# Start-up in half maxima with low parts last, rank products three units later, tokens picked inside the first expert's down stage

## The chip, the cores and the metric

One core of a Trainium2 chip runs the kernel in one launch. The metric is the device time of one execution in microseconds (us).

## The reference

Only the lines that set the work are kept. Q, K and V are 4 batches x 8 heads x 768 x 64. A row of Q sees only the rows of K whose nearest of 16 centroids is the same one. The result, 3072 tokens of 512 features, goes through a mixture of 16 experts in 4 groups (F = 1024), one expert per token.

```
q_assign = np.argmax(np.einsum('bhsd,hcd->bhsc', q_n, c_n), axis=-1)
k_assign = np.argmax(np.einsum('bhsd,hcd->bhsc', k_n, c_n), axis=-1)
mask = q_assign[:, :, :, None] == k_assign[:, :, None, :]
scores = np.where(mask, scale * np.matmul(q, k.transpose(0, 1, 3, 2)), -1e9)
attn = softmax(scores); x = attn @ v            # per head, then heads side by side
g_idx = np.argmax(x @ w_group, axis=1)          # group, then expert in the group
e_idx = np.argmax(xg @ w_expert[g], axis=1)
out[tok] = g_w * e_w * (np.maximum(x[tok] @ w1[g, e], 0.0) @ w2[g, e])
```

## The kernel before

Every number is split into a high and a low f16 part, so that a product is three matmuls (high by high, high by low, low by high). Four stages matter here.

**Start-up (lines 450 to 480).** Heads go in pairs; pair 0 is loaded first. `split` makes the high part of K and of Q on ACT (L178) and the low part on DVE (L187). The centroids are normalised, transposed on PE and split on DVE into CH and CL (L168, L169). `assign` multiplies the pair with CH and CL (L239, 72 matmuls) and finds the winning centroid of each row on DVE: L244 (maximum), L246, L247, L249, L251. `mask_now` transposes the resulting one-hot rows on PE (L276) and copies them into the operand tiles A, on ACT for Q (L278) and on DVE for K (L280). From then on the mask is part of the score product.

**Attention loop (lines 504 to 515).** 32 heads x 9 units. A **coarse** unit multiplies high parts only (L302, one bank of 512 columns) and DVE reduces it to row maxima (L305). When the 9 coarse units of a head are done, `rowmax` joins them (DVE L311, ACT L313), transposes the result on PE (L318 for heads 0 and 1) and writes it into A on ACT (L319). Only then can the head's **fine** units run: PE L342 and L343, exp on ACT (L347), low part of the exponentials on POOL (L349), products with V on PE (L368, L369) five units later. The coarse units run ahead of the fine ones by 13 units at first and by 18 later. A table of jobs keyed by unit number (`at`, `go`, `turn`) says when loads, splits, assignments, masks and routing of other heads are issued between units.

**Routing (lines 617 to 676).** At the end of each batch, `decide` chooses group and expert on DVE (L624 to L646), then counts ranks within the experts with 12 small matmuls on PE (L651 to L655), and turns them into positions on DVE (L658 to L663); POOL scatters token numbers and gates into `table` (L674). For batches 0 to 2 this runs as a job beside attention, and the value it yields (`yield PSM, 1, 1`) says how many units later it goes on. After batch 2 the first expert's known tokens are read from the table (tabA), cast to indices (DVE L838) and gathered (POOL L912). Batch 3 goes the way `early`, after attention.

**First expert (loop in the code below).** `part_a` runs the first expert on 288 tokens: eight up products (L950), then four down blocks d0 to d3 (L968, 24 matmuls each: 8 with hh and wh, 8 with hh and wl, 8 with hl and wh). Each up product yields once and each down block twice, after 12 and 24 matmuls; the loop counts those steps. At step `SLOTS` it issues `slots`: 6 f32 matmuls of `tb` (the table read back, SP L1084) by a permutation (L1114), which give the indices (DVE L1025) for the gathers of the next group of tokens (POOL L912). At step `SLT` it issues `tokens_b`: 48 matmuls that pick the expert's remaining tokens from batch 3 (L1096) and 6 f32 ones for their numbers (L1100); 128 tokens then follow as the second pass of this expert (L950).

Of the kernel before, what the change touches and what calls it, by code (L numbers as in the profile page):

```python
# [32 lines left out]
def attention(ctx, tc, qT, kT, vr, cen, R, DEN, cfg):  # L33
# [15 lines left out]
    AHEAD, AHEAD0 = 18, 13  # L49
# [116 lines left out]
    for j in range(2):  # L166
        r = slice(64 * j, 64 * j + 64)
        nc.vector.tensor_copy(out=CH[r, :, j], in_=cv[r, :, j])  # L168
        nc.vector.tensor_tensor(out=CL[r, :, j], in0=cv[r, :, j], in1=CH[r, :, j], op=ALU.subtract)  # L169


    def split(p, w, pool=False):
# [5 lines left out]
        nc.scalar.activation(out=hi, in_=x, func=AF.Copy, scale=SQ)  # L178
# [38 lines left out]
    def splitv(p, pool=False):  # L217
        x = st[p][2]
        vt = V[p % 4]
        nc.scalar.activation(out=vt[:, :, :, 64:128], in_=x, func=AF.Copy, scale=SQ)  # L220
        lo_part(vt[:, :, :, 0:64], x, vt[:, :, :, 64:128], pool)

    def assign(p, psum=None):
# [10 lines left out]
        for c in range(NCH):  # L234
            cs = slice(c * P, c * P + P)
            for t in range(2):
                hi, lo = st[p, t]
                for i, (a, m) in enumerate(((hi, CH), (hi, CL), (lo, CH))):
                    nc.tensor.matmul(out=sim[:, c, t], lhsT=a[:, cs], rhs=m[:, pr].rearrange("p h c -> p (h c)"), start=i == 0, stop=i == 2)  # L239
        sim = simt[:, 0:NCH * 4 * C].rearrange("p (g c) -> p g c", c=C)  # L240
        G = 4 * NCH
        yield
# [28 lines left out]
    def mask_now(h, pool):  # L271

        for t, dst in ((0, QA[h]), (1, KA[h])):
# [3 lines left out]
            if t == 0:  # L277
                nc.scalar.activation(out=dst[64:64 + C], in_=tp[64:64 + C, :S], func=AF.Copy, scale=-32768.0)  # L278
            else:
# [12 lines left out]
    def coarse(h, u, pool=(ps_c, "psc")):  # L292
# [6 lines left out]
        pc = pool[0].tile([P, 512], F32, name=pool[1])  # L299
        off = 0  # L300
# [6 lines left out]
    def rowmax(h):  # L307

        mp = cparts.pop(h)
        m7 = sm.tile([P, NCH], F32, name="m7")  # L310
        last["max"] = nc.vector.tensor_reduce(out=m7, in_=mp.rearrange("p j a x -> p (j a) x"), axis=AX.X, op=ALU.max)  # L311
        mh = ozs[0][:, 0, h, :, 64 + C] if h < 2 else sm.tile([P, NCH], F16, name="mh")
        nc.scalar.activation(out=mh, in_=m7, func=AF.Copy, scale=-1.0 / (SQ * SQ))  # L313
        if h < 2:

            tp = ps_f.tile([P, 512], F32, name="psf").bitcast(F16)
            for c in range(NCH):
                nc.tensor.transpose(out=tp[0:OZ, c * P:(c + 1) * P], in_=ozs[0][:, 0, h, c], identity=ident)  # L318
            nc.scalar.activation(out=QA[h][64:OZ], in_=tp[64:OZ, :S], func=AF.Identity, scale=oscale[64:OZ], bias=obias[64:OZ])  # L319
# [130 lines left out]
    split(0, 1)  # L450
    split(0, 0)
# [3 lines left out]
    run(assign(0, ps_f.tile([P, 512], F32, name="psf")))  # L455
    mask_now(0, (ps_o, "pso"))
    spread(0, (0,), part=(1,))
    banks = itertools.cycle(((ps_c, "psc"), (ps_f, "psf")))
    for u in range(9):
        coarse(0, u, next(banks))  # L460
    mask_now(1, (ps_o, "pso"))
    spread(0, (1,), part=(1,))
    run(rowmax(0))
# [5 lines left out]
    with tc.issue_after(last["mm"].ins), tc.issue_after(last["max"].ins):  # L469
        for u in range(AHEAD0 - 9):  # L470
            coarse(1, u, next(banks))
# [953 lines left out]
```

## Time and profile before

| | |
|---|---|
| median of 3 runs | 786.41 us (784.92 to 787.25) |
| profiled execution | 782.34 us, span of the core 780.6 us |
| PE busy | 733.3 us (94%) |
| PE weight loads | 626.5 us (80%, beside PE) |
| DVE busy | 612.0 us (78%) |
| POOL busy | 495.6 us (63%) |
| ACT busy | 466.8 us (60%) |
| DMA | 128.28 MB, mean 164 GB/s |

The span is the time on the core; the execution's own time is 1.74 us longer. A time of an instruction is its start from the span's beginning, and what stands in brackets behind it is the idle time of its engine just before it with what ended that. The clock column of the views by stretch is the clock granted to PE, where 1.00 is 2.4 GHz and 0.50 is 1.2 GHz.

### The profile page before, as it was taken

To read this page: it belongs to the slowest core of one execution; us is meant where nothing else is said; L and a number is where in the kernel's file an instruction comes from. 1 tells how busy PE (TensorE), PEld (TensorE's weight loads), DVE (VectorE), ACT (ScalarE), POOL (GpSimd) and SP (SyncE) were. 2 spreads that over 40 slices of the span, in tenths; PEclk is the share of its full clock that TensorE was granted. 3 is DMA by queue.
4 is the path that set the end of the run, shared out by engine and by line. 5 is a ranking of instruction groups with operands and counts; after the bars stand their busy time and mean duration, and the time that the engine had idled before them with its cause. 6 is when DMAs were issued, how large, how long until landed. Compare 5 with 4: busy or idle time off the path is not lost. (4 is left out here: it accounts for less than half of the span.)

```text
span 780.6 us, 26678 instructions
## 1 busy us (share of the span) xinstructions
PE 733.3 (94%) x11086; PEld 626.5 (80%) x11086; DVE 612.0 (78%) x1209; ACT 466.8 (60%) x910; POOL 495.6 (63%) x497
## 2 busy tenths in 40 slices
PE   5899999999999999998999799999999999999991
PEld 3677888878888788886878677887789999999991
DVE  5998879899798988988875465867789888888830
ACT  5567877768777687775895255444344444555530
POOL 9578787778977788776972445434564655565330
PEclk7899999999999999999999999999999999999996
DMA  8856534435344352223312397866688688889600
GB/s 244 204 144 168 148 102 119 137 94 148 104 119 134 94 149 68 55 94 127 92 30 84 85 313 239 272 224 217 209 265 257 218 259 277 285 255 300 194 32 17
DMA packets 80392, 128.28 MB, mean 164 GB/s; under 512 B 8851, under 2 KB 47251, under 8 KB 80264
## 3 DMA queue, kind: packets, MB, share of 16 engines
q1 hardware_dynamic: 74492, 113.12, 48.9%
q0 software_dynamic: 5616, 13.35, 4.9%
q8 instruction: 88, 1.44, 0.8%
q14 instruction: 40, 0.33, 0.1%
q10 hardware_dynamic: 156, 0.03, 0.0%
HBM read 93.20 MB, written 14.11 MB: 137 GB/s over the span
## 5 line engine op out<-in xcount | busy, mean ns | idle before, releaser
L349 POOL TENSOR_TENSOR pl<-p 128x512 f16<-128x512 f32 x278 | 287.3, 1052 | 84.9 <-ACT p L347 80.7
L305 DVE TENSOR_REDUCE mpart<-psc 128x1 f32<-128x512 f32 (+1 forms) x282 | 189.8, 682 | 35.0 <-PE psc L302 32.8
L347 ACT ACTIVATE p<-psf 128x512 f32<-128x512 f32 x288 | 168.7, 595 | 56.1 <-PE psf L343 49.1
L368 PE MATMUL pso<-V,p 128*128 128x65 f16 x1152 | 161.6, 193 | 0.0
L368 PE MATMUL pso<-V,pl 128*128 128x65 f16 x1152 | 161.2, 194 | 0.0
L369 PE MATMUL pso<-V,pl 128*128 128x64 f16 x1152 | 161.0, 191 | 0.0
L369 PE MATMUL pso<-V,p 128*128 128x64 f16 x1152 | 160.8, 191 | 0.0
L342 PE MATMUL psf<-A 82*128 82x384 f16 (+2 forms) x576 | 143.7, 275 | 4.2 <-ACT p L347 2.8
L343 PE MATMUL psf<-B 128*128 128x384 f16 (+2 forms) x576 | 143.7, 274 | 0.0
L369 PEld LDWEIGHTS <-p 128*128 128x128 bf16 x1152 | 112.6, 98 | 21.4 <-issue 0.2
L368 PEld LDWEIGHTS <-p 128*128 128x128 bf16 x1152 | 112.2, 97 | 9.3 <-issue 1.4
L369 PEld LDWEIGHTS <-pl 128*128 128x128 f16 x1152 | 112.8, 98 | 0.7 <-issue 0.4
L302 PE MATMUL psc<-A 80*128 80x512 f16 (+1 forms) x376 | 108.4, 330 | 5.1 <-DVE mpart L305 3.3
L368 PEld LDWEIGHTS <-pl 128*128 128x128 f16 x1152 | 111.2, 97 | 0.3
L953 DVE SCALAR_TENSOR_TENSOR hl<-psh,hh 128x160 f16<-128x160 f32 (+14 forms) x136 | 49.9, 370 | 58.6 <-ACT hh L952 50.4
L952 ACT ACTIVATE hh<-psh 128x160 f16<-128x160 f32 (+14 forms) x136 | 46.6, 347 | 65.7 <-PE psh L950 64.3
L950 PE MATMUL psh<-xT,wh0a 128*128 128x288 f16 (+7 forms) x512 | 74.7, 255 | 0.0
L1011 POOL DMA_INDIRECT out_dram<-y,ri x32 | 38.5, 1203 | 55.1 <-ACT y L1010 48.8
L912 POOL DMA_INDIRECT xg<-xbuf,ri x32 | 43.5, 1359 | 39.8 <-PE psm L922 25.7
L343 PEld LDWEIGHTS <-B 128*128 128x128 f16 x576 | 56.6, 98 | 13.7 <-issue 5.3
L950 PE MATMUL psh<-xT,wh0b 128*128 128x272 f16 (+6 forms) x448 | 65.2, 254 | 0.9 <-ACT xT L924 0.5
L342 PEld LDWEIGHTS <-A 82*128 82x128 f16 x576 | 55.5, 98 | 12.0 <-DMA A<-mr 0.7
(308 smaller groups left out, 1776.9 us busy)
## 6 DMA issues: line engine op xcount, KB each, us to landing
st<-w SPq DMA_DIRECT2D x128, 512.0 KB
B<-parts SPq DMA_DIRECT2D x64, 192.0 KB
kx<-kT SPq DMA_DIRECT2D x16, 384.0 KB
qx<-qT SPq DMA_DIRECT2D x16, 384.0 KB
vx<-vr SPq DMA_DIRECT2D x16, 384.0 KB
A<-parts SPq DMA_DIRECT2D x32, 192.0 KB
xbuf<-xs SPq DMA_DIRECT2D x4, 1536.0 KB
A<-mk SPq DMA_DIRECT2D x56, 24.0 KB
```

What stands on the lines that cost most here:

```text
L302: last["mm"] = nc.tensor.matmul(out=pc[:, off:off + k1 - k0], lhsT=QA[h % 8][0:80, c * P:(c + 1) * P], rhs=KA[h % 8][0:80, k0:k1], start=T ...
L305: nc.vector.tensor_reduce(out=(mp[:, 0, 0:1], mp[:, :, 1], mp[:, 1, 0:1])[i], in_=pc.rearrange("p (a x) -> p a x", a=n), axis=AX.X, op=ALU ...
L342: nc.tensor.matmul(out=o, lhsT=KA[h % 8][0:82, ks], rhs=QA[h % 8][0:82, q0:q1], start=True, stop=False)
L343: nc.tensor.matmul(out=o, lhsT=KBs[h][:, ks], rhs=QBs[h][:, q0:q1], start=False, stop=True)
L347: cfg["exp"] = nc.scalar.activation(out=p32, in_=pf, func=AF.Exp, scale=QK / (SQ * SQ))
L349: lo = (nc.vector if u in (EARLY if h < 2 else DVE_LO[h % 8] if h < NH - 2 else DVE_END) else nc.gpsimd).tensor_tensor(out=pl, in0=p32, in ...
L368: nc.tensor.matmul(out=O[:, col:col + 65], lhsT=p[:, bs], rhs=vh, start=c == 0 and q == 0 and i == 0, stop=False, skip_group_check=True)
L369: nc.tensor.matmul(out=O[:, col:col + 64], lhsT=p[:, bs], rhs=vl, start=False, stop=c == NCH - 1 and i == 1, skip_group_check=True)
L912: self.got = nc.gpsimd.indirect_dma_start(out=xg[0:n].rearrange("p a d -> p (a d)"), out_offset=None, in_offset=bass.IndirectOffsetOnAxis( ...
L950: self.mm = nc.tensor.matmul(out=ph[:, 0:M], lhsT=w[:, k, fs], rhs=xT[:, a, k], start=i == 0, stop=i == 3 * KD - 1)
L952: nc.scalar.activation(out=hh[:, f], in_=ph[:, 0:M], func=AF.Relu)
L953: self.ev = nc.vector.scalar_tensor_tensor(out=hl[:, f], in0=ph[:, 0:M], scalar=0.0, in1=hh[:, f], op0=ALU.max, op1=ALU.subtract)
```

## The change

The low parts of pair 0 go behind the four CH and CL instructions on DVE. `assign(0)` does its products in the order high by CH, high by CL, low by CH, K ahead of Q, and its chain of maxima once for each head of the pair, on half the columns each, with the mask transposes of head 0 between. Six matmuls on a zero tile (128x512) follow its products, and two more stand ahead of each of the first five coarse units: 16 matmuls and their weight loads are new on PE. Of head 0 only five coarse units come ahead of the loop; its row maximum is taken in two halves, and the first three fine units need the first half only. The other coarse units, `assign(1)`, and the masks of heads 2 and 3 become jobs of the first units; the number of coarse units ahead is 5 at first and grows by one with each unit up to 18. The mask of K for head 1 goes from DVE to ACT. The high parts made by `split` and `splitv` inside the loop are put behind the latest exp on ACT.

The rank products of batches 0 to 2 come three units after their inputs were issued instead of one. `SLOTS` goes from 11 to 13 and `SLT` from 13 to 8.

```diff
-    AHEAD, AHEAD0 = 18, 13
+    AHEAD = 18
...
-        nc.vector.tensor_tensor(out=CL[r, :, j], in0=cv[r, :, j], in1=CH[r, :, j], op=ALU.subtract)
+        last["cl"] = nc.vector.tensor_tensor(out=CL[r, :, j], in0=cv[r, :, j], in1=CH[r, :, j], op=ALU.subtract)
...
-        nc.scalar.activation(out=hi, in_=x, func=AF.Copy, scale=SQ)
+        with tc.issue_after(cfg["exp"].ins) if "exp" in cfg else ExitStack():
+            nc.scalar.activation(out=hi, in_=x, func=AF.Copy, scale=SQ)
...
+        if p == 0:
+
+            prods = [(c, t, i) for i in range(3) for t in (1, 0) for c in range(NCH)]
+        else:
+            prods = [(c, t, i) for c in range(NCH) for t in range(2) for i in range(3)]
+        for c, t, i in prods:
...
+        yield
+        if p == 0:
+
+            sim = simt[:, 0:NCH * 4 * C].rearrange("p (g h c) -> p g h c", h=2, c=C)
+            G = 2 * NCH
+            for h in range(2):
+                mx = sm.tile([P, 2 * G], F32, name="mx")[:, 0:G]
+                nc.vector.tensor_reduce(out=mx, in_=sim[:, :, h], axis=AX.X, op=ALU.max)
...
+                yield
+            return
...
             if t == 0:
                 nc.scalar.activation(out=dst[64:64 + C], in_=tp[64:64 + C, :S], func=AF.Copy, scale=-32768.0)
+            elif h == 1:
+                nc.scalar.activation(out=dst[64:64 + C], in_=tp[64:64 + C, :S], func=AF.Identity, scale=mscale[64:64 + C], bias=mbias[64:64 + C])
...
-    def coarse(h, u, pool=(ps_c, "psc")):
+    def coarse(h, u, pool=(ps_c, "psc"), idle=0):
...
+        for _ in range(idle):
+
+            nc.tensor.matmul(out=pc, lhsT=wz[:, 0:P], rhs=wz, start=True, stop=True)
...
-    def rowmax(h):
+    def rowmax(h, c0=0, c1=NCH):
...
-    split(0, 1)
-    split(0, 0)
+    with tc.issue_after(last["cl"].ins):
+        split(0, 1)
+        split(0, 0)
...
-    run(assign(0, ps_f.tile([P, 512], F32, name="psf")))
+    first = assign(0, ps_f.tile([P, 512], F32, name="psf"))
+    next(first)
+    with tc.issue_after(last["sim"].ins):
+        warm(6)
+    next(first)
     mask_now(0, (ps_o, "pso"))
+    run(first)
     spread(0, (0,), part=(1,))
     banks = itertools.cycle(((ps_c, "psc"), (ps_f, "psf")))
-    for u in range(9):
-        coarse(0, u, next(banks))
+    for u in range(5):
+        coarse(0, u, next(banks), 2)
+    run(rowmax(0, 0, NCH // 2))
     mask_now(1, (ps_o, "pso"))
     spread(0, (1,), part=(1,))
-    run(rowmax(0))
...
-    with tc.issue_after(last["mm"].ins), tc.issue_after(last["max"].ins):
-        for u in range(AHEAD0 - 9):
-            coarse(1, u, next(banks))
-        run(assign(1))
-        spread(1)
-        mask_now(2, (ps_m, "psm"))
-        mask_now(3, (ps_m, "psm"))
+    at(1, go, 1, assign(1))
+    at(2, spread, 1)
+    at(4, mask_now, 2, (ps_m, "psm"))
+    at(5, mask_now, 3, (ps_m, "psm"))
...
-    g, n = 0, AHEAD0
+    g, n = 0, 5
...
-            while n < min(9 * NH, g + 1 + min(AHEAD, AHEAD0 + g // 4)):
+            while n < min(9 * NH, g + 1 + AHEAD, 2 * g + 7):
                 coarse(n // 9, n % 9)
-                if n % 9 == 8:
+                if n == 8:
+                    run(rowmax(0, NCH // 2, NCH))
+                elif n % 9 == 8:
                     at(g + 1, go, g + 1, rowmax(n // 9))
...
-        yield PSM, 1, 1
+        yield PSM, 1 if early else 3, 1
...
-    SLOTS = 11
-    SLT = 13
+    SLOTS = 13
+    SLT = 8
```

Three places show what moves. DVE at start-up, before, from the low parts of pair 0 (parts) to the first coarse reduce:

```order
L187 SCALAR_TENSOR_TENSOR parts<-qx,parts 128x768
L168 CAST CH<-psm 64x4x16
L169 TENSOR_TENSOR CL<-psm,CH 64x4x16
L168 CAST CH<-psm 64x4x16
L169 TENSOR_TENSOR CL<-psm,CH 64x4x16
L244 TENSOR_REDUCE mx<-psf 128x24
L246 TENSOR_TENSOR psf<-psf,mx 128x384
L247 TENSOR_TENSOR psf<-psf,desc 128x384
L249 TENSOR_REDUCE mw<-psf 128x24
L251 TENSOR_TENSOR st<-psf,mw 128x6x2x16 x2
L280 TENSOR_SCALAR A_165<-pso 16x768
L305 TENSOR_REDUCE mpart_198<-psc 128x1
```

The same place in the change, from the second low part on (lines are later by 1 to 36 in the changed file):

```order
L188 SCALAR_TENSOR_TENSOR parts<-qx,parts 128x768
L252 TENSOR_REDUCE mx<-psf 128x12
L254 TENSOR_TENSOR psf<-psf,mx 128x12x16
L255 TENSOR_TENSOR psf<-psf,desc 128x12x16
L576 TENSOR_SCALAR WR<-wf 128x80
L257 TENSOR_REDUCE mw<-psf 128x12
L577 SCALAR_TENSOR_TENSOR WR<-wf,WR 128x80
L259 TENSOR_TENSOR st<-psf,mw 128x6x16 x2
L252 TENSOR_REDUCE mx<-psf 128x12
L254 TENSOR_TENSOR psf<-psf,mx 128x12x16
L255 TENSOR_TENSOR psf<-psf,desc 128x12x16
L307 TENSOR_SCALAR A_165<-pso 16x768
```

CH and CL now stand ahead of both low parts, the chain is there twice with half the columns, and two instructions on the router's weights (WR, before at L540 and L541, issued among the first jobs of the loop) now stand inside the first half chain; the K mask of head 0 (L307) stands inside the second one, ahead of its last two steps.

DVE behind the expert choice of the first batch, before: `rps` (L658) is the first reader of the rank products, `parts` with 384 columns (L199) a low part of a later pair.

```order
L643 TENSOR_REDUCE res<-rss 128x6
L305 TENSOR_REDUCE mpart_198<-psc 128x1
L644 TENSOR_SCALAR res<-res 128x6
L645 SCALAR_TENSOR_TENSOR res<-rse,res 128x6
L658 TENSOR_TENSOR rps<-psm,cb 128x96
L646 RECIPROCAL pay<-res 128x6
L199 TENSOR_TENSOR parts<-psm,parts 128x384
L305 TENSOR_REDUCE mpart_198<-psc 128x2
L382 TENSOR_SCALAR DEN<-pso 128x6
```

In the change:

```order
L680 TENSOR_SCALAR res<-res 128x6
L681 SCALAR_TENSOR_TENSOR res<-rse,res 128x6
L682 RECIPROCAL pay<-res 128x6
L335 TENSOR_REDUCE mpart_198<-psc 128x2
L413 TENSOR_SCALAR DEN<-pso 128x6
L415 RECIPROCAL rec<-DEN 128x6
L418 TENSOR_TENSOR pso<-pso,rec 128x6x64
L335 TENSOR_REDUCE mpart_198<-psc 128x1
L420 TENSOR_TENSOR xs<-pso,xs 128x6x64
L694 TENSOR_TENSOR rps<-psm,cb 128x96
```

`rps` is now behind two more coarse reduces and the normalising of a head (DEN, rec, pso, xs), and the low part has left this stretch for a later one.

PE in the first expert's down stage, before, between the last matmul of d1 and the first of d2:

```order
L968 LDWEIGHTS wh_10391
L968 MATMUL psy<-hl,wh_10391 128x288
L1114 MATMUL psm<-perm,tb 128x16 x6
L968 LDWEIGHTS wh_10391
L968 MATMUL psy<-hh,wh_10391 128x288
```

In the change, within d0, the end of `tokens_b` ahead of the fifth matmul by wl:

```order
L1132 LDWEIGHTS xs
L1132 MATMUL psm<-o_11499,xs 128x128
L1136 MATMUL psm<-pb,st 128x2 x6
L1004 LDWEIGHTS wl_10426
L1004 MATMUL psy<-hh,wl_10426 128x288
```

All 48 matmuls of L1132 (the last is shown) and the six of L1136 have moved ahead of half of d0 and of d1 and d2; the six of `slots` (L1150) stand behind d2, where `tokens_b` was.

## Rows read from the trace of the kernel before

**Rows 1.** The page: busy time of each engine, share of the span, instructions.
```profile
PE 733.3 (94%) x11086; PEld 626.5 (80%) x11086; DVE 612.0 (78%) x1209; ACT 466.8 (60%) x910; POOL 495.6 (63%) x497
```

**Rows 2.** Start by stretches (us): engines' busy time (instructions), PE clock, DMA share, GB/s.
```profile
15.00:18.00 3.00, 2.97 (x16) 1.98 (x16) 2.30 (x5) 0.37 (x1) 2.76 (x4) 0.50 0.93 230
18.00:19.00 1.00, 1.00 (x9) 0.74 (x8) 1.00 (x2) 0.97 (x2) 1.00 (x1) 0.74 0.56 175
22.00:28.00 6.00, 5.71 (x26) 3.41 (x27) 5.13 (x11) 2.64 (x5) 1.10 (x11) 0.50 0.78 215
...
36.00:42.00 6.00, 4.19 (x70) 3.09 (x69) 6.00 (x12) 1.83 (x4) 0.04 (x1) 1.00 0.64 161
42.00:52.00 10.00, 9.92 (x177) 7.96 (x174) 9.81 (x20) 6.72 (x11) 10.00 (x9) 1.00 0.79 220
```

**Rows 3.** Timeline of DVE: start, duration, instruction, idle before it.
```profile
7.26 0.95 DVE L187 SCALAR_TENSOR_TENSOR parts<-qx,parts 128x768 f16<-128x768 f32 x1
...
10.28 0.56 DVE L244 TENSOR_REDUCE mx<-psf 128x24 f32<-128x384 f32 x1 [1.19 <-PE psf L239]
...
14.83 0.56 DVE L280 TENSOR_SCALAR A<-pso 16x768 f16<-16x768 f16 x1 [1.40 <-PE pso L276]
16.08 0.69 DVE L305 TENSOR_REDUCE mpart<-psc 128x1 f32<-128x512 f32 x1 [0.70 <-PE psc L302]
16.69 0.68 DVE L305 TENSOR_REDUCE mpart<-psf 128x2 f32<-128x512 f32 x1
...
29.47 0.56 DVE L540 TENSOR_SCALAR WR<-wf 128x80 f16<-128x80 f32 x1
...
30.49 0.58 DVE L541 SCALAR_TENSOR_TENSOR WR<-wf,WR 128x80 f16<-128x80 f32 x1
```

**Rows 4.** Timeline of PE: first mask transposes, first coarse products, first fine product.
```profile
13.21 1.50 PE L276 MATMUL pso<-ident,st 128*82 128x128 f16 x12 [2.97 <-DVE st L251]
...
16.26 0.63 PE L302 MATMUL psc<-A 80*128 80x512 f16 x1
16.69 0.63 PE L302 MATMUL psf<-A 80*128 80x512 f16 x1
...
25.45 0.52 PE L342 MATMUL psf<-A 82*128 82x384 f16 x1
```

**Rows 5.** PE's groups, 40 to 420 us: busy, mean ns, idle before and releasers.
```profile
L592 PE MATMUL psm<-ident,xs 128*128 128x128 f16 x180 | 14.9, 219 | 0.9 <-DVE idA L838 0.6
...
L651 PE MATMUL psm<-roe,low 128*128 128x96 f16 x3 | 0.6, 203 | 3.8 <-DVE roe L639 3.8
```

**Rows 6.** Timeline of DVE at tabA.
```profile
394.46 0.15 DVE L838 CAST idA<-tabA 128x1 int32<-128x1 f32 x1 [0.68 <-DMA tabA<-table]
...
395.05 0.15 DVE L838 CAST idA<-tabA 128x1 int32<-128x1 f32 x1 [0.38 <-DMA tabA<-table]
```

**Rows 7.** Later stretches, columns as in rows 2.
```profile
152.00:168.00 16.00, 14.53 (x268) 11.78 (x267) 15.78 (x41) 9.91 (x22) 11.42 (x12) 1.00 0.32 80
...
449.00:452.00 3.00, 3.00 (x15) 1.85 (x13) 1.56 (x2) 0.27 (x1) 2.39 (x3) 0.50 0.95 367
```

**Rows 8.** Timeline of PE: down stage of the first expert, and gathered tokens' first transposes.
```profile
443.19 1.14 PE L968 MATMUL psy<-hl,wh 128*128 128x288 f16 x8
445.98 0.99 PE L1114 MATMUL psm<-perm,tb 16*128 16x16 f32 x7 [1.65 <-DMA tb<-table]
...
450.28 2.00 PE L968 MATMUL psy<-hl,wh 128*128 128x288 f16 x8
452.12 2.84 PE L1096 MATMUL psm<-o,xs 128*128 128x128 f16 x48
454.80 1.18 PE L1100 MATMUL psm<-pb,st 128*128 128x2 f32 x9
...
464.94 1.35 PE L922 MATMUL psm<-ident,xg 128*128 128x128 f16 x24
```

**Rows 9.** Timeline of POOL: the third of six gathers of the next tokens.
```profile
451.86 0.89 POOL L912 DMA_INDIRECT xg<-xbuf,ri  x1 [0.30 <-issue]
```

More of the change, by code (lines that the diff above doesn't have):

```diff
@@ L219, in splitv @@
         vt = V[p % 4]
-        nc.scalar.activation(out=vt[:, :, :, 64:128], in_=x, func=AF.Copy, scale=SQ)
+        with tc.issue_after(cfg["exp"].ins) if "exp" in cfg else ExitStack():
+            nc.scalar.activation(out=vt[:, :, :, 64:128], in_=x, func=AF.Copy, scale=SQ)
         lo_part(vt[:, :, :, 0:64], x, vt[:, :, :, 64:128], pool)
@@ L233, in assign @@
         sim = simt[:, 0:NCH * 4 * C].rearrange("p (c t x) -> p c t x", c=NCH, t=2)
[L234 to L239, printed above, removed]
+        if p == 0:
[3 more added lines that the diff above has]
+        for c, t, i in prods:
+            hi, lo = st[p, t]
+            a, m = ((hi, CH), (hi, CL), (lo, CH))[i]
+            last["sim"] = nc.tensor.matmul(out=sim[:, c, t], lhsT=a[:, c * P:c * P + P], rhs=m[:, pr].rearrange("p h c -> p (h c)"), start=(c, t, i) == prods[0] if p == 0 else i == 0, stop=(c, t, i) == prods[-1] if p == 0 else i == 2, skip_group_check=p == 0)
+        yield
[5 more added lines that the diff above has]
+                nc.vector.tensor_reduce(out=mx, in_=sim[:, :, h], axis=AX.X, op=ALU.max)
+                eq = sim[:, :, h]
+                nc.vector.tensor_tensor(out=eq, in0=eq, in1=mx.broadcast_to([P, G, C]), op=ALU.is_ge)
+                nc.vector.tensor_tensor(out=eq, in0=eq, in1=desc[:, 0:G], op=ALU.mult)
+                mw = sm.tile([P, 2 * G], F16, name="mw")[:, 0:G]
+                nc.vector.tensor_reduce(out=mw, in_=eq, axis=AX.X, op=ALU.max)
+                for t in (1, 0):
+                    last["oh"] = nc.vector.tensor_tensor(
+                        out=ohs[t][:, :, h],
+                        in0=eq.rearrange("p (c t) x -> p c t x", t=2)[:, :, t],
+                        in1=mw.rearrange("p (c t) -> p c t", t=2)[:, :, t].broadcast_to([P, NCH, C]),
+                        op=ALU.is_equal)
+                yield
+            return
         sim = simt[:, 0:NCH * 4 * C].rearrange("p (g c) -> p g c", c=C)
         G = 4 * NCH
-        yield
         mx = sm.tile([P, G], F32, name="mx")
```

11 lines of the change are left out of this document (6 added, 5 removed).

## The prediction

> **What bounds the kernel now.** First the page's busy times: PE works 733.3 us of a span of 780.6 [rows 1], so only some 47 us, in which PE stands or waits, and the time it spends at half clock, can be won without taking PE work out. The change takes none out; it adds 16 matmuls. So the second view is the one by stretches, to see where PE is idle or slow, and which engine is full there. At the start it is DVE: from 36 to 42 us it is busy 6.00 of 6.00 while PE does 4.19, from 42 to 52 it is busy 9.81 of 10 [rows 2], and PE's clock is 0.50 (1.2 GHz) from 15 to 18 and again from 22 to 28. Third, the timelines of that start [rows 3, 4]: DVE's first coarse reduce comes at 16.08, PE's first fine product at 25.45. Fourth, PE's groups between 40 and 420 us: among the waits the change touches, PE stood 3.8 us for the rank inputs (roe) and 0.6 for the indices idA [rows 5]. Last, the down stage of the first expert: PE stands 1.65 us for the table read, and then runs at half clock [rows 7, 8]. Behind it PE is the bound to the end, and the change moves nothing there.
>
> All durations come from the profiled execution, 782.34 us, which is 4.1 below the median of 786.41; I take the sum of gains from the median.
>
> **Start-up, up to the first coarse reduce.** Before, the low parts end at 8.21 (7.26 + 0.95), CH and CL follow, then PE's products, and DVE idles 1.19 us until the maximum at 10.28 [rows 3]. With CH and CL first, only the last third of the products (low by CH) waits for the low parts. DVE does the same work ahead of the maximum; the idle 1.19 shrinks to some tenths, but CH and CL now wait for the centroids' transposes in turn, which the low parts covered: a gain of 0 to 1, I take 0.5. The chain itself is 12 half-size steps for 6; the mask transposes of head 0 (12 in 1.50 us [rows 4]) can start after half of it, which would win about 1 us. Against that stand the two WR instructions, 0.56 and 0.58 [rows 3], now inside the first half: 1.14 us, most of the win. So the first reduce stays near 16, between 15 and 16.5.
>
> **Start-up, from there to 57 us.** DVE is the bound, so its work counts. Gone from this stretch: WR, 1.14, and a K mask now on ACT, 0.56 [rows 3]; added: a second short maximum, 0.17 as an estimate (the whole one has 18 values a row, this one 9; a like-sized one took 0.15 [rows 6]). Net 1.5. DVE's own idle time from 22 to 28 and 42 to 52 is 0.87 + 0.19 = 1.06 [rows 2], part of which goes because fine units can start after 5 coarse units and half a maximum: 4 reduces at a pitch of 0.61 [rows 3] less ahead of the first fine product, and half the transposes and copies, so near 21.5 rather than 25.45. This gives ACT, POOL and PE work earlier, but the coarse units that are taken out of the front come back between the fine ones, on the same full DVE; hence I do not count those 4 us as won. Upper end 1.5 + 1.06 = 2.6. Lower end: two idle matmuls stand ahead of each of the last two of the five coarse units with DVE waiting behind them. At half clock a 512-column matmul takes 0.43 (16.26 to 16.69 [rows 4]), so such a unit takes three, 1.29, against a reduce each 0.61: 1.4 us for the two units; the 12 transposes of head 1 ahead of the sixth unit add 1.50 - 0.61 = 0.9. That makes 1.5 - 2.3 = -0.8. At full clock both vanish. Forecast for the whole start 1.7 us, nearer the upper end, since before PE reached 0.74 already from 18 to 19 [rows 2] with less to do, and now six idle matmuls (2.6 us at 0.43) fill the wait during the maxima.
>
> By a rule of the Trainium skill (TensorE: Matmul & The Clock Gate, Part 4: PE-mode transpose) transposes do not count as work that brings the full clock; by it the masks' 12 and 12 transposes would leave all of that to the 16 idle matmuls and the coarse products, and the start would be worth the lower end, -0.8. The trace does not contradict it: the clock is 0.50 through 15 to 18, with transposes and the first coarse units mixed [rows 2].
>
> **Rank products.** Three waits of 1.27 on average, 3.8 in all [rows 5]. Two more units now lie between inputs and products, and the products' readers are behind two more reduces on DVE. PE is freed, but DVE is busy 15.78 of 16.00 us in this stretch [rows 7], so PE may meet it again at the next coarse unit. Two low parts at least leave the stretch (0.56 each in the 384-column form; an estimate from the 0.56 that DVE's 384-column steps take [rows 3]), so what DVE allows is 0.22 + 1.1 = 1.3 of the first wait, while its plain slack alone would allow 0.22. Ends 0.7 (three times 0.22) and 3.8; I take 2.4, nearer to the wait that the trace names than to the slack, since 18 coarse units are in hand.
>
> **The price of it.** The scatter of each batch comes two units later. For batch 2 the read of the table (tabA) is due then: DVE stood 0.68 + 0.38 for it [rows 6], of which PE lost 0.6 [rows 5]. With the gap one unit shorter, DVE would stand about a unit longer. Ends 0 (other jobs cover it) and 1.4 (a whole unit: 288 of them lie between 25.45 and 443.19 [rows 4, 8], under 1.45 each); I take -0.8, by the share of its wait that PE lost so far (0.6 of 1.06).
>
> **Tokens and slots.** With slots behind d2, the table read has 4 us of tokens_b (2.84 + 1.18 [rows 8]) and two down blocks more; the stall of 1.65 goes. It was followed by 0.50 of the clock from 449 to 452 [rows 7], in which 8 matmuls took 2.00 us against 1.14 before the stall [rows 8]: 0.86 for 8, 16 of them, 1.7 us. Without the idle PE should keep the clock. tokens_b's inputs were finished on DVE and ACT before the down stage begins, and its results are read in the second pass. Ends 1.6 (stall only) and 3.4; I take 3.3. What is late next are the gathers: each starts some 4 to 5 us later, and the first 24 transposes of the gathered tokens stand at 464.94, while the third gather's issue ended at 452.75 [rows 8, 9]. With the transposes now at some 461.6 and that issue ending at 457.5, 4 us are left for landing, so I cost it at nothing; if the cover is gone, PE waits what is missing, an estimate of 1 to 2 us.
>
> **Sum.** 1.7 + 2.4 - 0.8 + 3.3 = 6.6 us: 779.8 on the median, 775.7 on the profiled execution. All lower ends give -0.8 + 0.7 - 1.4 + 1.6 = 0.1, all upper ends 2.6 + 3.8 + 0 + 3.4 = 9.8.
>
> **The rivals.** (a) The start is worth nothing or less: the idle matmuls stand in DVE's way at half clock, -0.8 instead of 1.7. For it: the clock was 0.50 from 22 to 28 behind a run of small products [rows 2], and the change keeps such runs. This is also where the rule on transposes (the Trainium skill, TensorE: Matmul & The Clock Gate, Part 4: PE-mode transpose) would lead. Against: six idle matmuls more during the chain. Gain 4.1, 782.3 us. (b) All upper ends meet: ranks, idA and the clock go free at once. For it: the waits are named in the rows; against: DVE full at both places. 776.6. (c) No change that shows: DVE takes back the ranks (0.7), the clock dips in the down stage whatever stands there (1.6), and the start loses 0.8, the read costs 0.8: gain 0.7, 785.7. For it: DVE's 15.78 of 16. Against: all three have to happen. (d) Slower, by the clock at the start: with five coarse units instead of thirteen ahead, PE works in short pieces between DVE's reduces and never earns the full clock before the loop runs evenly. It had 0.50 up to 28 [rows 2]. In the 42 to 52 stretch PE is busy 9.92 of 10 at 1.00 [rows 2], so each us there at 0.50 costs half a us. It decides if half clock lasts to about 47: 18 us past 29 cost 9, more than 6.6 + 2.4. If it lasts to 50 the time is 786.4 - 6.6 + 10.5 = 790.3. Against: before it came up by itself once fine units ran, and they now run sooner.
>
> **Chances.** The forecast, 4.5 to 9 us of gain, has 0.50; (a) 0.18; (b) 0.14; (c) 0.10; (d) 0.08. What a measurement of this kernel can tell from no change is about 0.3%, 2.4 us. Forecast, (a) and (b) are faster by more than that: 0.82; (c) is the same: 0.10; (d) slower: 0.08. The range takes in (a), (b) and most of (c), with a us for the median: 774.8 to 786.2.
>
> **What would show it.** Right: no wait of PE for roe in the groups and no new wait for coarse maxima near 157 of like size; the table read no longer in front of PE, granted clock 1.00 through the down stage; first coarse reduce near 16, first fine product near 21.5, and the unit that was at 57 us some 1.7 earlier; DVE's waits for tabA longer by about a us. Wrong: clock 0.50 past 29; PE standing for xg behind the second pass; the idle matmuls followed by DVE waits; PE's idle time moved from roe to mpart or pl.

## The result, and the profile after

The changed kernel takes **793.54 us** (median of 6 runs, 790.19 to 794.47) against 787.2 us for the kernel before, measured beside it (6 runs): a ratio of 1.0102, 95% interval 1.0069 to 1.0135. It is slower by 6 to 8 us where 6.6 us less was forecast. The profiled execution has a span of 791.1 us; that of before, 780.6 us, lies at the low end of its runs, so the traces differ by more (10.5 us) than the medians. Where one trace is set against another, I use the places at which the distance changes.

The page: PE is busy 5.7 us more than in [rows 1]. 3.9 of that falls before 22 us, where the 16 new matmuls run, most of them at half clock.

```profile
PE 739.0 (93%) x11102; PEld 627.1 (79%) x11102; DVE 613.5 (78%) x1215; ACT 468.5 (59%) x913; POOL 495.4 (63%) x497
```

The start by stretches, columns as in [rows 2]:

```profile
15.00:18.00 3.00, 2.28 (x16) 1.71 (x15) 2.24 (x7) 0.80 (x1) 2.76 (x4) 0.50 1.01 358
...
22.00:28.00 6.00, 4.62 (x72) 3.30 (x71) 4.81 (x10) 4.72 (x9) 1.67 (x12) 0.99 1.00 219
...
36.00:42.00 6.00, 3.81 (x83) 3.14 (x80) 5.64 (x11) 2.38 (x3) 0.21 (x1) 1.00 0.28 69
42.00:52.00 10.00, 9.32 (x110) 6.44 (x111) 9.40 (x17) 6.33 (x11) 4.82 (x5) 0.83 0.68 181
```

DVE is no longer full from 36 to 52. The clock, which before stood at 0.50 from 22 to 28, is 0.99 there and falls later instead, to 0.83 on average from 42 to 52. The timeline of DVE, to be held against [rows 3]:

```profile
11.37 0.36 DVE L252 TENSOR_REDUCE mx<-psf 128x12 f32<-128x192 f32 x1 [1.55 <-PE psf L244]
...
12.91 1.43 DVE L577 SCALAR_TENSOR_TENSOR WR<-wf,WR 128x80 f16<-128x80 f32 x1
...
17.71 0.68 DVE L335 TENSOR_REDUCE mpart<-psc 128x1 f32<-128x512 f32 x1
...
402.22 0.15 DVE L874 CAST idA<-tabA 128x1 int32<-128x1 f32 x1 [3.75 <-DMA tabA<-table]
```

The first maximum comes 1.1 us later than before (10.28), the second WR instruction takes 1.43 us instead of 0.58, and the first coarse reduce comes at 17.71 instead of 16.08. The last row is the table read that [rows 6] show with 0.68. PE's timeline at the places of [rows 4, 8], and at the waits that are new:

```profile
10.77 0.21 PE L244 MATMUL psm<-CH,parts 128*128 128x32 f16 x1 [1.52 <-ACT parts L179]
...
17.00 0.58 PE L332 MATMUL psc<-A 80*128 80x512 f16 x1 [0.72 <-DVE A L307]
...
25.00 0.32 PE L373 MATMUL psf<-A 82*128 82x384 f16 x1
...
160.80 0.38 PE L332 MATMUL psc<-A 80*128 80x512 f16 x1 [0.26 <-DVE mpart L335]
...
167.02 0.38 PE L332 MATMUL psc<-A 80*128 80x512 f16 x1 [1.00 <-DVE mpart L335]
...
407.00 0.22 PE L355 MATMUL psm<-ident,mh 128*6 128x128 f16 x1 [3.42 <-DVE wl L820]
...
458.45 1.58 PE L1150 MATMUL psm<-perm,tb 16*128 16x16 f32 x12
...
470.92 0.27 PE L986 MATMUL psh<-xT,wh 128*128 128x128 f16 x2 [1.88 <-DVE hl L989]
```

The first row is a product of the next pair (it writes psm, pair 0 writes psf) that stands on PE ahead of pair 0's last products and waits for a high part of the next pair on ACT. The second row is the first coarse product; the two that [rows 4] show are the third and fourth of before, whose first stands at 15.43, so it comes 1.6 us later. Of the ten idle matmuls meant for the places ahead of the first five coarse units, PE had started six before 9 us; only four stand among the coarse units, at 18.23 and 19.51. The groups answer to [rows 5]: the 3.8 us for roe are gone, those for coarse maxima stand at 8.6, and 3.4 us are new.

```profile
L332 PE MATMUL psc<-A 80*128 80x512 f16 (+1 forms) x357 | 101.8, 326 | 9.4 <-DVE mpart L335 8.6
...
L355 PE MATMUL psm<-ident,mh 128*6 128x128 f16 x30 | 6.5, 218 | 3.6 <-DVE wl L820 3.4
...
L687 PE MATMUL psm<-roe,low 128*128 128x96 f16 x3 | 0.6, 204 | 0.0
```

To see where the distance between two traces arises, take the reciprocal that DVE issues once at the end of each head (L384 before, L415 after; heads count from 0, and a plus means later than before's trace). The changed kernel's lies 2.09 us behind after head 2, 0.65 after head 5, 2.29 after head 17, 3.98 after head 25, 3.32 after head 28, and 7.50 after head 29; 7.09 at the last head. So some of the distance grows by about 0.7 us per four heads, and 4.2 us come at once at the table read. The 2.09 us at head 2 do not yet show a loss at the start, since executions of one code differ by as much: tokens only, tokens first and tokens first with slots early (below) have before's code up to the first expert, and their head 2 ends at +0.78, +2.75 and +0.17. That loss shows in the medians of the start alone.

### The profile page after: what moved, and what is told of

Read it like the earlier page. It is cut to its first block, busy times and chain, and to the rows that moved or that the text cites. A ratio compares the mean times of both kernels' runs of the same rounds, so it can differ in the third digit from the quotient of the medians.

```text
span 791.1 us, 26752 instructions
## 1 busy us (share of the span) xinstructions
PE 739.0 (93%) x11102; PEld 627.1 (79%) x11102; DVE 613.5 (78%) x1215; ACT 468.5 (59%) x913; POOL 495.4 (63%) x497
## 5 line engine op out<-in xcount | busy, mean ns | idle before, releaser
L335 DVE TENSOR_REDUCE mpart<-psc 128x1 f32<-128x512 f32 (+1 forms) x286 | 193.1, 683 | 33.3 <-PE psc L332 31.8
L399 PE MATMUL pso<-V,pl 128*128 128x65 f16 x1152 | 163.9, 194 | 1.0 <-POOL pl L380 0.9
L400 PE MATMUL pso<-V,pl 128*128 128x64 f16 x1152 | 163.7, 192 | 0.0
L400 PE MATMUL pso<-V,p 128*128 128x64 f16 x1152 | 162.5, 192 | 0.0
```

What stands on the lines that cost most here:

```text
L335: nc.vector.tensor_reduce(out=(mp[:, 0, 0:1], mp[:, :, 1], mp[:, 1, 0:1])[i], in_=pc.rearrange("p (a x) -> p a x", a=n), axis=AX.X, op=ALU ...
L399: nc.tensor.matmul(out=O[:, col:col + 65], lhsT=p[:, bs], rhs=vh, start=c == 0 and q == 0 and i == 0, stop=False, skip_group_check=True)
L400: nc.tensor.matmul(out=O[:, col:col + 64], lhsT=p[:, bs], rhs=vl, start=False, stop=c == NCH - 1 and i == 1, skip_group_check=True)
```

## The experiments

Each kernel ran beside the kernel before on one chip; kernels measured together, four or two at a time, share the runs of before. Times are medians in us; the ratio is estimated from all runs and can differ from the quotient of the medians by some 0.2%.

| kernel | median | before beside it | ratio, 95% interval |
|---|---|---|---|
| tokens only | 784.59 | 786.21 | 0.9985 (0.9955 to 1.0015) |
| ranks only | 788.90 | 786.21 | 1.0041 (1.0011 to 1.0071) |
| start only | 792.31 | 786.21 | 1.0084 (1.0051 to 1.0117) |
| tokens first | 782.51 | 786.21 | 0.9973 (0.9939 to 1.0008) |
| start, no exp order | 792.75 | 785.79 | 1.0095 (1.0068 to 1.0123) |
| exp order only | 790.99 | 785.79 | 1.0075 (1.0049 to 1.0100) |
| ranks, two batches | 786.83 | 785.79 | 1.0001 (0.9979 to 1.0023) |
| start, no exp order, tokens first | 789.00 | 785.79 | 1.0059 (1.0030 to 1.0088) |
| start, exp order for 4 pairs | 788.30 | 783.36 | 1.0059 (1.0037 to 1.0080) |
| the same, tokens first | 786.08 | 783.36 | 1.0037 (1.0014 to 1.0061) |
| start, 4 pairs, no idle matmuls | 786.09 | 783.36 | 1.0025 (1.0002 to 1.0048) |
| exp order for 4 pairs, tokens first | 783.95 | 783.36 | 1.0007 (0.9988 to 1.0027) |
| chain only | 784.60 | 784.08 | 1.0014 (0.9994 to 1.0034) |
| exp order for 4 pairs only | 783.57 | 784.08 | 1.0006 (0.9991 to 1.0022) |
| tokens first, slots early | 782.22 | 784.08 | 0.9987 (0.9971 to 1.0003) |
| chain, tokens first | 785.01 | 784.08 | 1.0035 (1.0011 to 1.0059) |
| start pinned | 784.25 | 784.05 | 1.0014 (0.9993 to 1.0035) |
| start pinned, tokens | 783.52 | 784.05 | 0.9994 (0.9974 to 1.0014) |

"Exp order" is the rule that puts the high parts of `split` and `splitv` behind the latest exp. The three parts run alone make +0.41%, +0.84% and -0.15%, together +1.1%; the whole change makes +1.02%. Within intervals of some 0.3 points for each, they add.

**Ranks only.** The kernel before with one line changed.

```diff
-        yield PSM, 1, 1
+        yield PSM, 1 if early else 3, 1
```

> The kernel before with the rank products of batches 0 to 2 three units after their inputs instead of one. Theory A: PE's 3.8 us of waits for roe vanish, but half or more comes back as waits for coarse maxima, and the read of the table for the first expert comes too late, so DVE stands 3 to 4 us for tabA and PE as long: 1 to 4 us slower, 788 to 791, with the loss at the last but two head of batch 3. Theory B (the late tabA of the changed kernel comes from its start-up and its other order of jobs): tabA costs 1 us or less, 1 to 3 us faster, about 785.

Theory A held: +2.7 us. Its groups of PE, columns as in [rows 5]:

```profile
L302 PE MATMUL psc<-A 80*128 80x256 f16 (+1 forms) x355 | 101.2, 326 | 5.3 <-DVE mpart L305 4.7
...
L324 PE MATMUL psm<-ident,mh 128*6 128x128 f16 x30 | 6.5, 218 | 3.6 <-DVE wl L784 2.9 <-ACT mh L313 0.3
...
L651 PE MATMUL psm<-roe,low 128*128 128x96 f16 x3 | 0.6, 204 | 0.0
```

And where the first batch's wait went, in PE's timeline:

```profile
159.89 0.38 PE L302 MATMUL psc<-A 80*128 80x512 f16 x1 [0.27 <-DVE mpart L305]
...
166.11 0.38 PE L302 MATMUL psc<-A 80*128 80x512 f16 x1 [1.00 <-DVE mpart L305]
```

Before, PE waited 1.27 us for roe at 158.29 and 0.20 for a maximum at 165.31. Now it waits 0.27 + 1.00 for coarse maxima, up to 8 us later than for roe: nearly the same sum, as if DVE was behind by that much whatever PE did in the meantime. Over the loop 2.5 of the 3.8 us come back so (waits for maxima rise from 2.2 to 4.7), and the 2.9 us behind the late table come on top.

**Ranks, two batches.** As above, but batch 2, whose table the first expert reads, keeps one unit (`1 if early or b == self.B - 2 else 3`).

> The kernel before with the rank products three units late for batches 0 and 1 and one unit late for batch 2, whose table read the first expert waits for. Theory A (the whole cost of the rank shift is the late table, and its gain is given back as waits for coarse maxima): the 3.4 us in front of the first expert's tokens go, the waits for roe and mpart sum to the same as before, and the time is that of before within a us, 786. Theory B (freed rank waits are a gain): 1.5 to 2.5 us faster, 784.

Ratio 1.0001. The 2.9 us in front of the matmul on mh are gone, and nothing is won. The groups:

```profile
L302 PE MATMUL psc<-A 80*128 80x256 f16 (+1 forms) x355 | 101.2, 326 | 5.1 <-DVE mpart L305 4.8
...
L651 PE MATMUL psm<-roe,low 128*128 128x96 f16 x3 | 0.6, 204 | 1.3 <-DVE roe L639 1.3
```

4.8 + 1.3 is the 2.2 + 3.8 of before to 0.1 us. So the rank shift is worth nothing that these runs can tell, and its price is the late table.

**Start only.** The changed kernel with the ranks at one unit, SLOTS 11 and SLT 13.

> The changed kernel with the rank products one unit after their inputs again and with SLOTS 11, SLT 13: the start-up and the splits behind exp alone. Theory A: the first heads end about 1 us later than before, and each four heads lose another 0.5 us where high parts of a later pair wait behind the latest exp: 3 to 4 us slower at the end of attention, about 791. Theory B (the start itself costs about 1 us, and what grows afterwards belongs to the rank products): about 788, with a constant distance to before after the fifth head.

+6.1 us, the largest part. Its profiled execution was the shortest of its six runs (788.17), so the trace shows less than the median: heads 5, 9, 17 and 25 end at -1.54, -0.68, +0.96 and +3.00 us against before. The growth belongs to this part, as theory A said.

**Start without exp order, and exp order only.** The first is start only with the condition taken out of both places, as below; the second is the kernel before with the condition put in.

```diff
-        with tc.issue_after(cfg["exp"].ins) if "exp" in cfg else ExitStack():
+        if True:
```

> The start-up alone (rank products, SLOTS and SLT as before), and the high parts no longer put behind the latest exp. Theory A (the ordering behind exp moves DVE's low parts against the coarse maxima and so costs about 0.9 us in each four heads): the distance to before stays constant after the third head, waits of PE for mpart fall from 6.1 to near before's 2.2 us, and the time is 3 to 5 us below that of the start-up with it (792.3): 787 to 789. Theory B (the loss grows because the start-up leaves another phase between coarse and fine units): the same growth of 0.9 us per four heads and about 792.

> The kernel before with only the high parts of split and splitv put behind the latest exp. Theory A: PE's waits for mpart rise by about 4 us, the distance to before grows by 0.9 us in each four heads from the third quarter of batch 0 on, and the time is 789 to 791. Theory B (the phase after the start-up is the cause): no growth, 786 to 787.

Theory A held for the growth and failed for the time. Without the order the distance is flat: +5.96 at head 5 and +5.55 at head 25. With the order alone in the old kernel it grows from -0.78 to +7.83 between the same heads, and the time is 5.2 us longer. PE's groups of that kernel:

```profile
L304 PE MATMUL psc<-A 80*128 80x256 f16 (+1 forms) x355 | 101.7, 327 | 7.7 <-DVE mpart L307 7.2
...
L653 PE MATMUL psm<-roe,low 128*128 128x96 f16 x3 | 0.6, 215 | 4.8 <-DVE roe L641 4.8
```

Waits for maxima rise from 2.2 to 7.2 us, those for roe from 3.8 to 4.8: 6.0 of the 8.6 us by which the distance grows. But the start without the order is no cheaper (+7.0): it loses all of it by head 2. So the order helps the new start and harms the loop. The same start with tokens first as well takes 789.00, 3.2 above before; the two pieces had been expected at 781 to 783 if both were a gain, and at 785 or more if the start is a loss of its own, which it is.

**Start with exp order for four pairs.** The condition gets `and p < 4`; then SLT 8 as well. Pairs 0 and 1 are split before the first exp, so it acts on pairs 2 and 3 alone.

> The start-up alone (rank products, SLOTS and SLT as before) with the ordering behind exp kept for the first four pairs and dropped for all later ones. Theory A (the ordering is worth some us in the start-up and costs 0.9 us per four heads later): the start of the run with it (head 5 at -1.5 to +0.7 against before's trace), and a constant distance from there on; time 786 to 789, some 4 below 792.3. Theory B (the start-up costs 5 to 6 us by itself, whatever the ordering): 791 to 793.

> The kernel of the run above with SLT 8 as well (tokens first, slots as before). If the parts add: 3 us below it, 783 to 786; if the start-up or the end takes it back: no difference to it.

The distance is flat behind head 2 in both, and PE's waits for maxima are near before's:

```profile
L332 PE MATMUL psc<-A 80*128 80x512 f16 (+1 forms) x357 | 102.5, 328 | 2.8 <-DVE mpart L335 2.8
```

+4.9 us still, between the two theories; with tokens first 2.2 less. The two have the same start, yet head 2 ends at +6.08 in one trace and at +0.39 in the other. The stretch from 15 to 22 of the first, then of the second:

```profile
15.00:22.00 7.00, 6.28 (x35) 3.98 (x34) 5.21 (x11) 1.07 (x2) 6.76 (x18) 0.50 1.07 245
```

```profile
15.00:22.00 7.00, 5.59 (x70) 3.74 (x69) 6.62 (x16) 3.11 (x5) 6.76 (x17) 1.00 0.96 246
```

Twice as many PE instructions at full clock. But the clock is not the whole of the 5.7 us between these two executions: head 0 ends 2.1 us apart (+4.54 and +2.41), and 3.6 more come between heads 1 and 2. There, in the first, ACT stands in front of the first high part of pair 5, one of those that the condition leaves out:

```profile
67.01 0.84 ACT L179 ACTIVATE parts<-qx 128x768 f16<-128x768 f32 x1 [2.65 <-issue]
```

The load of its Q was issued at 60.81. The trace names no releaser; before's trace names a load at the same job (1.01 us for K of pair 5, at 60.19). PE then waits 2.09 and 0.70 us for exp, which stands behind it on ACT. The second trace has 0.66 us of idle at this place, the two kernels without any order 2.27 us each. In the changed kernel, whose coarse units began at half clock as in the first, the same high part comes 11.6 us later, long after its load, and ACT does not stand in front of it; head 2 ends at +2.09:

```profile
78.62 0.84 ACT L179 ACTIVATE parts<-qx 128x768 f16<-128x768 f32 x1
```

So the order behind exp also keeps ACT from standing for a late load. How much of the start's loss is the clock and how much this stand, no run separates.

**No idle matmuls.** The four-pairs kernel with `coarse(0, u, next(banks))` and without `warm(6)`. (The expectation compares it with the start as first measured; the kernel has the order for four pairs, so it stands beside that one.)

> The start-up alone, as first measured (792.3), without its 16 matmuls on the zero tile. Theory A (they bring PE's full clock earlier, and a start at half clock costs 2 to 3 us): granted clock 0.50 until 22 us or later, first coarse reduce near 17 with the second five units slower, time 793 to 795. Theory B (they only stand in the way of the coarse units): DVE's waits between the first coarse reduces go, 1 to 2 us faster, 790 to 791.

Theory B's sign: 2.2 us faster than with them (786.09 against 788.30, measured together; the means of the twelve runs each differ by 2.4, with an interval of about 1.0 to 3.8 worked out from the runs). Its PE ran the first coarse units at half clock (0.63 each). With the idle matmuls they ran at full clock (0.38) in two of six traces, and at half in four: the clock came early now and then, and on the median the matmuls cost more than that gave. Without them the start is still 2 to 3 us above before.

**Chain only.** CH and CL first, maxima in halves, K mask on ACT; thirteen coarse units ahead and the rest as before.

> The kernel before with only the first piece of the start-up: low parts of pair 0 last, maxima in halves, K mask of head 1 on ACT. Thirteen coarse units ahead, the whole row maximum of head 0, no idle matmuls and no ordering behind exp, as before. Theory A (what costs in the start-up is that only five coarse units stand ahead, so that assign, masks and the other coarse units follow between the first fine units on a full DVE, and PE falls to half clock a second time): no such loss here, head 2 within 1.5 us of before's traces, time within 1.5 us of before. Theory B (the halved chain with the two WR instructions inside delays everything): head 2 at +2 to +4, 2 to 4 us slower.

> The first piece of the start-up (as in the chain-only run) and SLT 8. If both pieces are worth what the theories say: 3 to 4 us below before; if the chain costs, at the chain-only run less 2 to 4 us.

Theory A for the first: no change. Its DVE:

```profile
10.07 0.36 DVE L252 TENSOR_REDUCE mx<-psf 128x12 f32<-128x192 f32 x1 [0.44 <-PE psf L244]
...
15.27 0.68 DVE L335 TENSOR_REDUCE mpart<-psc 128x1 f32<-128x512 f32 x1
```

The chain works: the first coarse reduce is 0.8 us earlier than before (16.08) and 2.4 earlier than in the changed kernel. Here PE does not wait for the next pair ahead of the maximum, and WR stands later. The 0.8 us are gone by head 2 (+2.11), though that is no more than executions of before's code differ by. With tokens first the ratio is 0.35% above before, 0.9 us on the medians, which neither theory gave; one of its twelve runs, 792.17, stands far off the others, and I have no cause for it.

**Start pinned.** The kernel without idle matmuls, with the first products of pair 1 put behind the exp of their unit and WR behind the first row maximum; then SLT 8 and SLOTS 9 as well.

```diff
+        with tc.issue_after(last["mm"].ins), tc.issue_after(cfg["exp"].ins):
+            next(g1)
...
+        with self.tc.issue_after(self.cfg["lastmax"].ins):
```

> The new start-up without idle matmuls and with the ordering behind exp for the first four pairs (2.7 us slower than before when it ran without pins), with two placements mended: the first products of pair 1 (assign) no longer stand ahead of the low-by-CH products of pair 0 on PE, and the two WR instructions stand behind the first half of the row maximum on DVE. Theory A (these two placements are what the new start-up loses: 1.3 us and 1.4 us ahead of the first coarse reduce): first maximum near 10.1 instead of 11.3, first coarse product near 14.6 instead of 17.5, time 0 to 3 us below before. Theory B (the loss is made later, where assign, masks and coarse units follow between fine units): the first coarse product comes as early, and head 2 still ends 1.5 us or more after before's; 1 to 3 us slower than before.

> The kernel of the run above with SLT 8 and SLOTS 9 (1.9 us below before when they ran alone): the best of the pieces. If they add and theory A holds: 2 to 5 us below before, 780 to 782; if theory B holds: at before within 1.5 us.

DVE of the first:

```profile
10.27 0.36 DVE L252 TENSOR_REDUCE mx<-psf 128x12 f32<-128x192 f32 x1 [0.44 <-PE psf L244]
...
15.46 0.68 DVE L335 TENSOR_REDUCE mpart<-psc 128x1 f32<-128x512 f32 x1
```

The places came as theory A said, and the first fine product is at 22.05 instead of 25.45. In time, the medians go from 2.7 us behind before to 0.2, but the two were measured at different times and the ratios, 1.0025 and 1.0014, have intervals that overlap: that the two placements account for the rest is likely and not shown. Nothing is won either. Head 2 ends at +1.68 here and at +0.44 in the kernel with tokens, so where the early fine units are given back is not settled; that DVE has the same work to do is the reason I would expect.

**Tokens.** SLOTS 13 and SLT 8; SLT 8 alone; SLT 8 and SLOTS 9.

> The kernel before with only the two step numbers of the first expert changed (SLOTS 13, SLT 8). Theory A (each part acts by itself): the down stage gets about 4 us shorter, as in the changed kernel's trace, and the second pass gives back more, because the gathers of the next tokens start some 8 us later than before and meet the weight loads: PE stands 3 to 6 us between the second pass and the use of the gathered tokens. Net 2 to 4 us slower, about 790. Theory B (the stalls behind the second pass come from the shift of the attention loop against the weight stream, not from the two numbers): 3 to 4 us faster, about 783.5.

> The kernel before with SLT 8 alone: the tokens are picked inside d0, but the slots stay between d1 and d2, so the gathers start about when they did. Theory A: the table read has 4 us more time, the stall of 1.65 and the half clock behind it go, and the gathers meet the weight loads no later than before: 3 to 4 us faster, about 783.5, and no stall behind the second pass. Theory B (PE stands behind the second pass whenever the down stage is shorter, since weights or instructions arrive no earlier): no change, 786 to 788, with the 4 us standing between the second pass and the gathered tokens.

> SLT 8 and SLOTS 9: tokens inside d0, slots already between d0 and d1. Theory A (what the down stage wins is given back because the gathers of the next tokens come too late for the second pass): gathers start 2 us earlier against PE's work than with SLOTS 11 and the time is 1 to 2 us below that of tokens first (ratio 0.9973): 4 to 5 us below before. Theory B (weights and instruction supply limit the second pass): the same as tokens first, 2 to 4 us below before, or the table read stalls PE again for 1 us.

1.6, 3.7 and 1.9 us faster on the medians, the interval of each ratio reaching past 1.0. In the first, the stall at the table read is gone, and PE stands after it in the second pass:

```profile
462.98 0.30 PE L950 MATMUL psh<-xT,wh 128*128 128x128 f16 x2 [1.92 <-issue]
```

With slots early the table read stalls PE again, longer than in before's trace (1.65), and the time is no worse:

```profile
446.49 1.86 PE L1114 MATMUL psm<-perm,tb 16*128 16x16 f32 x8 [2.58 <-DMA tb<-table]
```

At the old places the stall comes out as long in other traces: 2.61 us in ranks only, 2.90 with the start pinned. So neither theory is shown; the places of slots and tokens matter by 0 to 4 us, and the supply around 460 to 475 us varies between executions: even ranks only, whose first expert is that of before, lost 3.8 us between the last head and 521 us against before's trace.

**Exp order for four pairs in the old start**, with tokens first and alone.

> The kernel before with the ordering behind exp for the first four pairs only, and SLT 8. Theory A: the ordering helps the old start-up by up to 1 us (head 5 at -0.8 where it was applied to all pairs), tokens first gives 2 to 4: 781 to 784. Theory B (the ordering helps only the new start-up): as tokens first alone, 782.5.

> The kernel before with the ordering behind exp for the first four pairs and nothing else. Theory A (the ordering is harmless in the old start-up): within 1 us of before, head 5 between 0 and +1. Theory B (it hides what tokens first gains in the run that had both): 2 us slower.

Both are at before (1.0007 and 1.0006). The order is harmless there, and tokens first, 3.7 us better when first measured alone, shows nothing here. Against the same kernel without it, it took 3.8 us less in the start without the order, 2.2 less in the start with four pairs, and 0.4 more behind the chain; that gain is not settled. No version beats the kernel before by more than the measurement can tell; tokens first with slots early comes nearest, with an interval of 0.9971 to 1.0003.

## Why the prediction was wrong

**Start-up, +1.7 us of gain forecast, 6.1 of loss measured.** Three steps failed. The first coarse reduce was put "near 16, between 15 and 16.5"; it came at 17.71. I costed the chain by its instructions on DVE and left out who feeds it. PE's order had two products of pair 1 ahead of pair 0's last twelve, waiting 1.52 us for ACT; and WR was taken at 0.56 and 0.58, from a place where POOL did something else, and took 0.20 and 1.43. The first fine product, put near 21.5, came at 25.00. Pinning both away brought the reduce to 15.46 and the fine product to 22.05. Second, the idle matmuls: I took them as fillers that would bring the full clock, and the lower end (-0.8) as unlikely. They cost 2.2 us on the median, and in the changed kernel's trace PE still ran at half clock from 15 to 22. This was rival (a), with the right mechanism and too small a price. Third, the order behind exp: the prediction did not cost it at all beyond the start. PE's waits for coarse maxima rise from 2.2 to 6.1 us in the start-only trace; DVE's order there has the later pairs' low parts among the maxima, which I take for the cause. The group before, then in start only:

```profile
L302 PE MATMUL psc<-A 80*128 80x256 f16 (+1 forms) x355 | 101.0, 325 | 2.2 <-DVE mpart L305 2.2
```

```profile
L332 PE MATMUL psc<-A 80*128 80x512 f16 (+1 forms) x356 | 101.9, 327 | 6.6 <-DVE mpart L335 6.1
```

The change applies it to three high parts of each of the pairs that are split inside the loop, pairs 2 to 15, and I treated it as part of the start. By the ratios the new start costs 0.84% as it is, 0.59% with the order kept to four pairs, 0.25% without the idle matmuls as well, and 0.14% with the two placements pinned, each figure within some 0.2 to 0.3 points. What makes up the last two is not told apart.

By the rule of the Trainium skill (TensorE: Matmul & The Clock Gate, Part 4: PE-mode transpose) the masks' transposes would not help the clock. The traces agree in so far as the clock stayed at 0.50 through both groups of 12 in the changed kernel; that they are the reason is not shown, since the idle matmuls around them did not raise it there either, and in two traces of the same start (start only; four pairs with tokens first) the clock is 1.00 from 15 to 22, with the second group at 18.53.

**Rank products, 2.4 us of gain forecast, none found.** The lower reasoning, DVE's slack of 0.22 us of 16 [rows 7], was the right one, and I set it aside because 18 coarse units were in hand. Those do not help: PE takes the coarse units in a fixed order and has two banks for them, so it meets a late DVE at the next reduce. With two batches shifted, the freed waits came back as waits for mpart of the same sum (6.0 us for both kinds before, 6.1 then).

**The price, 0.8 us forecast, 2.7 measured alone.** The sign and the mechanism were right, the size was not. The scatter was moved by two units, and the job that reads the table by one. I priced the shift by the share that PE lost of a wait that was nearly covered (0.6 of 1.06). Past the cover DVE stands for all of it: 1.82 + 2.17 us for tabA in the ranks-only trace, and PE for 2.9.

**Tokens, 3.3 us of gain forecast, 1.6 measured alone, with an interval that takes in nothing and 3.5 (0.9955 to 1.0015).** The stall of 1.65 and the half clock went as said, and the down stage ended about 4 us closer. What stands behind it was costed at nothing, and that step failed: the gathers begin at 461.16 instead of 448.69, weights and gathers fill the DMA engines (share 1.03 to 1.11 from 467 to 471), and PE stands about 3 us there in the changed kernel. But it stands within the second pass, and no wait for xg is in front of the first transposes of the gathered tokens at 471.59; that the late gathers are the cause is not shown, and what PE waits for there stays open.

**The sum and the chances.** 82% for faster was too high because the terms were not independent: the start and the ranks both rested on DVE having room where the same rows showed it full. Slower had one rival, the clock lasting to 47 us, and that is not what happened. No rival named a wait that moves to the next consumer of the same engine, which is what the term of the ranks did. Two figures of the text do not come out: the 9 us of rival (d) equal 6.6 + 2.4 and are not more, and the lower end of the range, 774.8, lies 1.8 us below the sum of the upper ends (776.6), where the text names one.

## What to carry to other kernels

A wait that is removed on one engine is only won if the engine that was late has slack by the next meeting point; look for that meeting point, and if the late engine is 98% busy, expect the same sum of waits there. When instructions are given to a scheduler instead of a fixed place, read the new order on every engine that feeds the step, not only on the engine that it was meant for: here two small matmuls of another pair and two weight instructions took the lead of the reordered chain (first reduce at 17.71, against 15.27 without them). Look also for a step that waits for a load ahead of work that is ready: one such high part held ACT for 2.65 us and PE behind it. Price a delayed transfer by its whole delay beyond the cover, not by the share that was visible while it was nearly covered.

## What the runs showed of the hardware

The granted clock is not to be trusted at the start of an execution, before its first change there. The tokens-only kernel and the one with exp order for four pairs and tokens first have the old start; the stretch from 13 to 22 us reads 1.00 in the first and 0.50 in the second, with the same number of PE instructions in the same time:

```profile
13.00:22.00 9.00, 7.74 (x72) 5.53 (x72) 6.86 (x13) 2.45 (x3) 8.76 (x18) 1.00 0.90 199
```

```profile
13.00:22.00 9.00, 7.74 (x72) 5.53 (x72) 6.86 (x13) 1.60 (x2) 8.76 (x18) 0.50 0.75 187
```

The length of a coarse product of 512 columns tells: 0.63 us at half clock, in both, and 0.38 at full. The readings of the starts above agree with it.

The second WR instruction on DVE took 1.43 us from 12.91 while POOL ran a 1.58 us TENSOR_TENSOR from 12.65. It ended at 14.34, 0.1 us behind POOL's 14.23. Three other traces of the new start (start only, four pairs, no idle matmuls) have it from 13.01, 12.88 and 12.82, for 1.33, 1.45 and 1.53 us: it always ends within 14.33 to 14.35, whenever it starts. In the start without the order the first WR instruction starts at 12.71 and ends at 14.30, after 1.59 us. So in these traces either of them ends with POOL's step and not after a time of its own; pinned elsewhere the second took 0.23 us. No run took POOL's step away.

At PE's longest stand in the second pass (to 470.92) the only instruction packet of those 8 us began in the half microsecond from 470.0; that PE waited for it, behind weights and gathers, is read from one trace and not shown.
